# One-piece projections, a halved first block of x and a new table of thresholds in a two-attention kernel

## The chip, the cores and the metric

The kernel runs on one core of a Trainium2 chip. Five engines work side by side, each through its own queue in order: TensorE (PE) multiplies matrices into eight banks of PSUM, VectorE (DVE) and ScalarE (ACT) read those banks, GpSimd (POOL) works between on-chip tiles, and SyncE (SP) issues transfers. The metric is device time in microseconds (us) of one execution, the median of several. Before the change it is 1202.8 us in three runs (1199.12, 1202.80 and 1205.19).

## The reference, cut to what matters

Two attentions over 2048 positions and 512 features, each with 32 heads of 16 features, are computed from separate inputs, and their outputs stand side by side.

```python
# part A: softmax attention
q, k, v = split(x @ wqkv)                       # 32 heads of 16
p = softmax(q @ k.T * 16 ** -0.5)               # 2048 x 2048 for each head
a = concat_heads(p @ v) @ wo
# part B: linear attention with softmax feature maps
pq, pk = q @ w_phi, k @ w_phi                   # for each head 16 x 16
phi = lambda t: concat([softmax(t), softmax(-t)])
kv, z = phi(pk).T @ v, sum(phi(pk))
b = concat_heads(phi(pq) @ kv / (phi(pq) @ z + 1e-6)) @ wo
out = concat([a, b])
```

## The kernel before, in words

Part A is nearly all of the time. The work is cut into units: a group of four heads and 128 or 256 queries. There are eight groups, and each unit goes through three passes.

- **D pass.** `d_fill` multiplies keys with queries (line 971, 512 columns, half of PE's rows) into one PSUM bank, or two neighbouring banks at once. DVE then takes the maximum over the keys (line 1084): over one bank (512 elements, "128x1" in the profile, a single) or over two (1024 elements, "128x2", a pair). POOL joins the maxima (lines 1116 to 1122), and SP carries them by a transpose and two copies (lines 1134 and 1140) into the extra row of `QZ`, so that the next product already has the maximum taken off.
- **E pass.** `e_fill` multiplies again (line 1234), and ACT takes the exponential of one or two banks (line 1246) into a ring of tiles `pT`.
- **PV.** `pv_run` multiplies the exponentials with V (line 1324), four heads in four column strips of PE. A column of ones beside V gives the sums. The last three units take their sums with `ones_t` (line 1319) instead.

The projections of part A (`proj` and `proj8`), the output projection (`oproj`), and all of part B's matmuls are *jobs*: a list of pieces that PE runs between the passes. A piece is not broken up; between two pieces of a job passes may be put in. Before, a projection of four matmuls of 512 columns is two pieces of two.

The order of everything is set on the host while the program is built. A planner (`_Account`) keeps an account of when each engine comes free, by costs written in the code, and at each step chooses what each engine does next; what comes out is a fixed list of instructions for each engine, with the semaphore waits that the data need. What PE takes next depends on thresholds (`T`): above which lead of DVE and ACT a job's piece or PV may run (`COL`, `INCOL`), below which lead a single instead of a pair is taken (`SINGLE`, `ESINGLE`), when POOL, ACT and DVE share evacuations (`BAL`), and how busy PE must be kept (`UA`, `RF`, `LHARD`, `REPM`). Where PE would be too little busy by that account, the planner lets it repeat a D or E product (`again`) or multiply zeros (`fill_mm`, line 1854). The thresholds have one row for each 60 us of the account.

At the start, the first 512 rows of x come as two transfers (`load_x(0, ...)`, `load_x(1, ...)`). PE turns them by 16 matmuls with the identity (line 374) into four banks, one for each quarter of the features and 512 positions wide; then come two idle matmuls, and DVE and ACT evacuate two banks each (lines 381 and 383). The first projection of K and then that of Q (line 710) follow, 512 columns each; DVE makes the masked queries `QZ` of the first three units out of the bank of Q (line 734), and the D passes begin. From this point the planner orders everything.

## Time and profile before

| What | Value |
|---|---|
| Median of three runs | 1202.8 us |
| Time of the profiled execution | 1199.05 us |
| Its span, first to last instruction | 1197.3 us |
| DVE busy | 1170.3 us, 98% of the span |
| ACT busy | 1149.8 us, 96% |
| PE busy | 1117.4 us, 93% |
| POOL busy | 821.8 us, 69% |
| Granted TensorE clock, mean | 0.999 |

The profiled execution lies 3.75 us under the median of the runs. A row of the groups has line, engine, operation, tiles, shapes and count, then the busy time of all and the mean duration of one in ns, then the engine's idle time just before them. Instructions of one engine overlap a little at their ends, so durations of neighbours add up to more than the time between their starts. A row of the timeline has start, length, engine, line, what it does and how many follow each other; its shape is that of the first of them. A window row gives each engine's busy time within a stretch.

### The profile page before, as it was taken

The page shows a single profiled execution, that of the slowest core. Times are in us where ns is not written, and L with a number is a line of the kernel's source. Part 1 is how long each engine was busy: PE and PEld are TensorE (multiplying, and loading weights), DVE is VectorE, ACT ScalarE, POOL GpSimd, SP SyncE. Part 2 cuts the span into 40 slices and gives each one's busy share as a digit, 9 for nine tenths or more (in the row PEclk, how much of TensorE's full clock was granted, in tenths as well). Part 3 has the DMA queues.
Part 4 walks back from the last instruction along what each step waited for, and adds up shares of the span by engine and source line. Part 5 has one row for each costly group of instructions (what it writes and reads, how often), then busy time and mean ns, then how long its engine had stood idle before and what let it go on. Part 6 is the DMA issues. An engine that isn't in the chain of part 4 may idle for free.

```text
span 1197.3 us, 32106 instructions
## 1 busy us (share of the span) xinstructions
PE 1117.4 (93%) x13025; PEld 468.9 (39%) x13025; DVE 1170.3 (98%) x1290; ACT 1149.8 (96%) x1891; POOL 821.8 (69%) x1636
## 2 busy tenths in 40 slices
PE   8998999998999999999999998999999998899998
PEld 3433333343334333333433333333333333345555
DVE  8999999999999999999999999999999999999995
ACT  5898999999999999999999999999999999999997
POOL 8511211227888888888787887888888888888860
PEclk9999999999999999999999999999999999999999
DMA  5011221210002001001000101121112111111120
GB/s 142 9 25 43 42 48 32 43 38 8 8 14 35 8 6 26 13 10 22 12 7 17 25 7 22 22 49 31 29 34 33 35 34 27 20 29 37 33 30 18
DMA packets 104119, 33.61 MB, mean 28 GB/s; under 512 B 86692, under 2 KB 103972, under 8 KB 103972
## 3 DMA queue, kind: packets, MB, share of 16 engines
q1 hardware_dynamic: 102916, 31.31, 13.4%
q8 instruction: 102, 1.67, 0.6%
q14 instruction: 45, 0.37, 0.1%
q10 hardware_dynamic: 1056, 0.26, 0.1%
HBM read 5.26 MB, written 4.19 MB: 8 GB/s over the span
## 4 chain that ended last, share of the span: by engine, by line
ACT 38%; DVE 33%; PE 23%; SPq 2%; issue 1%; POOL 1%; DMA 1%
ACT pT L1246 32%; DVE part L1084 32%; PE PS L1234 7%; PE PS L971 6%; PE PS L1324 5%; PE PS L1419 2%; ACT eB L1639 1%; ACT xAT L560 1%; PE PS L777 1%; ACT zS L1011 1%; ACT X L560 1%; SPq L1392 1%; ACT WQp L560 1%; POOL uB L1588 1%; PE PS L1563 0%
## 5 line engine op out<-in xcount | busy, mean ns | idle before, releaser
L1084 DVE TENSOR_REDUCE part<-PS 128x2 f32<-128x1024 f32 (+1 forms) x1118 | 1130.0, 1079 | 7.6 <-PE PS L971 5.2
L1246 ACT ACTIVATE pT<-PS 128x512 bf16<-128x512 f32 (+1 forms) x1573 | 1027.7, 797 | 21.3 <-PE PS L1234 17.9
L1234 PE MATMUL PS<-QZ,KT 64*128 64x256 bf16 (+1 forms) x4906 | 560.4, 259 | 40.9 <-ACT pT L1246 22.0
L971 PE MATMUL PS<-KT,QZ 64*128 64x512 bf16 x2139 | 484.5, 383 | 26.3 <-DVE part L1084 9.7
L1234 PEld LDWEIGHTS PS<-QZ,KT 64*128 64x128 bf16 x4906 | 245.5, 94 | 323.1 <-ACT pT L1246 161.4
L971 PEld LDWEIGHTS PS<-KT,QZ 64*128 64x128 bf16 x2139 | 126.2, 93 | 198.2 <-DVE part L1084 72.2
L1324 PE MATMUL PS<-pT,VP 128*17 128x256 bf16 (+1 forms) x4672 | 186.7, 261 | 0.9
L1403 POOL TENSOR_TENSOR QT<-X,Yd 128x256 bf16<-128x256 f32 (+1 forms) x70 | 46.8, 668 | 95.4 <-DMA Yd<-Yd 95.1
L1324 PEld LDWEIGHTS PS<-pT,VP 128*17 128x17 bf16 x4672 | 74.9, 88 | 95.2 <-issue 79.0
L1588 POOL TENSOR_TENSOR uB<-uB 128x256 f32<-128x256 f32 (+2 forms) x160 | 83.4, 522 | 10.1
L1591 POOL TENSOR_SCALAR uB<-uB 128x256 f32<-128x256 f32 (+2 forms) x128 | 82.6, 646 | 11.2
L1116 POOL TENSOR_TENSOR dm<-part 128x16 f32<-128x16 f32 (+1 forms) x66 | 15.7, 238 | 91.1 <-DVE part L1084 90.8
L915 POOL TENSOR_TENSOR QZ<-QT,mask 128x512 bf16<-128x512 bf16 (+1 forms) x70 | 65.9, 941 | 15.7 <-PE PS L1234 12.8
L1645 POOL TENSOR_TENSOR xAT<-eB 128x512 f32<-128x512 bf16 x32 | 36.9, 1152 | 40.8 <-ACT eB L1639 40.6
L1677 POOL TENSOR_TENSOR wA<-eB,rB 128x1024 bf16<-128x1024 bf16 x32 | 61.7, 1928 | 2.0
L560 ACT ACTIVATE xAT<-PS 128x512 f32<-128x512 f32 (+3 forms) x83 | 50.1, 617 | 4.4 <-PE PS L1443 2.9
L1648 POOL TENSOR_TENSOR xAT<-xAT 128x256 f32<-128x256 f32 x64 | 36.0, 563 | 5.0
L1563 PE MATMUL PS<-WKp,xBT 128*128 128x512 bf16 x128 | 36.4, 383 | 1.1 <-ACT pT L1246 0.5
L1639 ACT ACTIVATE eB<-uB 128x1024 bf16<-128x1024 f32 x32 | 36.0, 1124 | 0.0
L1419 PE MATMUL PS<-WOp,QT 128*128 128x512 bf16 x120 | 35.8, 384 | 0.1
L1588 POOL TENSOR_TENSOR uB<-xAT,mB 128x512 f32<-128x512 f32 x32 | 33.8, 1057 | 1.8
L1662 POOL TENSOR_TENSOR WQp<-rB,WQp 128x64 f32<-128x64 f32 x96 | 30.6, 319 | 6.4
(113 smaller groups left out, 752.4 us busy)
## 6 DMA issues: line engine op xcount, KB each, us to landing
out_dram<-xAT SPq DMA_DIRECT2D x31, 128.0 KB, 1.8
Yd<-Yd SPq DMA_DIRECT2D x220, 16.0 KB, 2.1
QT<-eB SPq DMA_DIRECT2D x60, 32.0 KB, 2.0
QZ<-mcols SPq DMA_DIRECT2D x110, 1.0 KB
pT<-in_A_x_dram SPq DMA_DIRECT2D x3, 512.0 KB, 7.5
KT<-eB SPq DMA_DIRECT2D x48, 32.0 KB, 2.0
mcols<-stage SPq DMA_TRANSPOSE x69, 2.2
Yd<-Yd SPq DMA_DIRECT2D x60, 8.0 KB, 1.9
```

The costliest lines, as they stand in the source:

```text
L560: return P.op("act", lambda e: e.activation(dst, src, ACT.Copy), tk)
L915: "pool", lambda e: e.tensor_tensor(QZ[:, u % NQZ, :, 0:w], QT[:, g, q0:q0 + w].unsqueeze(1).broadcast_to([128, 2, w]), mask2[:, 0, :].uns ...
L971: return e.matmul(PS[:, b, :], QZ[p:p + 64, u % NQZ, r % 2, qt * 128:qt * 128 + 128], KT[p:p + 64, g, kc * 512:(kc + 1) * 512], start=star ...
L1084: tk = P.op("dve", lambda e: e.tensor_reduce(o, banks_ap(banks), AX.X, ALU.max), dep)
L1234: tok = P.op("pe", lambda e, r=rs[k], b=banks[k], kt=kt, x=x: e.matmul(PS[:, b, x * w:(x + 1) * w], KT[64 * (r // 2):64 * (r // 2) + 64, g ...
L1246: tk = P.op("act", lambda e: e.activation(pT[:, s0:s0 + n, :] if n > 1 else pT[:, s0, :], banks_ap(banks), ACT.Exp, scale=0.25), dep)
L1324: tok = P.op("pe", lambda e, r=r, kt=kt, x=x, s=es_[r][1]: e.matmul(PS[32 * r:32 * r + 17, bank, 0:w], VP[:, kt, 4 * g + r, :], pT[:, s, x ...
L1419: return e.matmul(PS[:, b, :], QT[:, i, st * 128:(st + 1) * 128], WOp[:, i, :], start=(i == 0), stop=(i == 7))
L1588: return P.op("pool", lambda e: e.tensor_tensor(o, a, b, op), dep)
L1591: return P.op("pool", lambda e: e.tensor_scalar(o, o, 0.0, None, ALU.max), dep)
L1639: cx["e"] = K.task("act", (0.95, 1.07), lambda eng: P.op("act", lambda e: e.activation(eB[:], uB[:], ACT.Exp), toks(d3)), d3, prio=-0.5, n ...
L1677: cx["phi"] = K.task("pool", (1.95, 1.95 + PLAT), lambda eng: P.op("pool", lambda e: e.tensor_tensor(phiB[k].rearrange("p (g f) -> p g f", ...
```

## The change

Four things are changed together.

1. Jobs of four matmuls that were two pieces of two become one piece of four: the eight-head projections of part A (`proj8`, 27 jobs), the feature maps of part B (`fm`, 32), the projection of V of part B (`v_job`, 16) and the output projection of part B (`ob_job`, 16). The projections in `proj` (the first K, Q and all V of part A) and `oproj` stay in pieces of two.
2. The first 512 rows of x are turned and evacuated in two halves of 256 positions, each after its own transfer, into eight banks in place of four. Q of the first 256 positions is projected by itself, right after the first half (four matmuls of 256 columns into bank 0), and `QZ` of the first two units is made from it; Q of the other 256 positions follows K as a job. The copy of the weights of Q into their padded place stands behind the first half of x on DVE. The two idle matmuls are gone.
3. The third transfer of x (`load_x(2, ...)`) waits until the first has landed. It is issued on SP's queue, and the weights and the later parts of x stand behind it there.
4. All 20 rows of the thresholds are replaced, and the account starts at 6.8 us in place of 7.6, with some arrival times moved by the same kind of amount.

```diff
-        def load_x(name, b0, b1):
+        def load_x(name, b0, b1, dep=()):
             t_xs[name] = P.dma("sp", dsem("xs%d" % name), lambda e: e.dma_start(
-                xs[:, b0:b1, :], A_x[0][128 * b0:128 * b1, :].rearrange("(b p) n -> p b n", p=128)))
+                xs[:, b0:b1, :], A_x[0][128 * b0:128 * b1, :].rearrange("(b p) n -> p b n", p=128)), list(dep))
...
-        load_x(2, 4, 8)
+        load_x(2, 4, 8, [t_xs[0]])
...
         pe_idle(6, [t_zmv, t_ones])
-        for rb in range(4):
+        t_x0 = {}
+        for hf in range(2):
+            for rb in range(2 * hf, 2 * hf + 2):
+                for ct in range(4):
+                    t_turn = P.op("pe", lambda e, rb=rb, ct=ct, hf=hf: e.matmul(
+                        PS[:, 4 * hf + ct, 128 * (rb % 2):128 * (rb % 2) + 128],
+                        xs[:, rb, ct * 128:ct * 128 + 128], ident[:, :],
+                        start=True, stop=True), [t_xs[hf], t_ident] if ct == 0 else [])
             for ct in range(4):
-                t_turn = P.op("pe", lambda e, rb=rb, ct=ct: e.matmul(
-                    PS[:, ct, 128 * rb:128 * rb + 128], xs[:, rb, ct * 128:ct * 128 + 128], ident[:, :],
-                    start=True, stop=True), [t_xs[rb // 2], t_ident] if ct == 0 else [])
-        pe_idle(2)
-        t_x0 = []
+                dst_x = xAT[:, ct, 256 * hf:256 * hf + 256]
+                src_x = PS[:, 4 * hf + ct, 0:256]
+                if ct % 2 == 0:
+                    t_x0[hf, ct] = P.op("dve", lambda e, o=dst_x, i=src_x: e.tensor_copy(o, i), [t_turn])
+                else:
+                    t_x0[hf, ct] = P.op("act", lambda e, o=dst_x, i=src_x: e.activation(o, i, ACT.Copy), [t_turn])
+            if hf == 0:
+                t_wqp = pad_copy(WQp, 0, t_wq0)
         for ct in range(4):
...
+            t_q0 = P.op("pe", lambda e, ct=ct: e.matmul(
+                PS[:, 0, 0:256], WQp[:, ct, 0, :], xAT[:, ct, 0:256], start=(ct == 0), stop=(ct == 3)),
+                [t_wqp, t_x0[0, 2], t_x0[0, 3]] if ct == 0 else [])
...
-            {'SINGLE': 1.013, 'ESINGLE': 1.026, 'ZBIAS': 0.274, 'DBIAS': 0.27, 'ZREST': 0.238},
+            {'SINGLE': 0.55, 'RF': 0.478, 'LHI': -0.049, 'JOBHOLD': 18.93, 'PVN': 2, 'ZBIAS': 0.053, 'ZREST': 0.028},
...
-        K.now = 7.6
+        K.now = 6.8
...
+                c0 = 256 if (kind, g, c) == ("q", 0, 0) else 0
...
+        held.add(0)
+        first_qz(0, T_q0, [0, 1])
         early = [("k", 0, 0), ("q", 0, 0)]
...
-            job(at, [(2, 512, mm), (2, 512, lambda e, b, i: mm(e, b, i + 2))], fin,
+            job(at, [(4, 512, mm)], fin,
                 T_xa[c] + [w8[kind]], prio)
...
-            job(K.now + 8.0, [(2, 512, mm), (2, 512, lambda e, b, i: mm(e, b, i + 2))], fin,
+            job(K.now + 8.0, [(4, 512, mm)], fin,
                 [BL[("xb", st // 4)], BL["wb"]], prio=K.now + 14)
```

Since the planner makes the whole order anew, nearly every row of every engine moves. The places that the prediction speaks of are these.

On PE, the start of the program. `pT` holds x as it came, `WKp` and `WQp` the weights of K and Q, `QZ` and `KT` are queries and keys of a D pass. Lines below 400 stand ahead of the planner. Before:

```order
L368 MATMUL PS<-zmv,ones_t 128x512 x6
L374 MATMUL PS<-ident,pT 128x128 x16
L368 MATMUL PS<-zmv,ones_t 128x512 x2
L710 MATMUL PS<-xAT,WKp 128x512 x4
L710 MATMUL PS<-xAT,WQp 128x512 x4
L807 MATMUL PS<-ident,pT 128x128 x12
L971 MATMUL PS<-KT,QZ 128x512 x4
L807 MATMUL PS<-ident,pT 128x128 x16
```

Now:

```order
L367 MATMUL PS<-zmv,ones_t 128x512 x6
L376 MATMUL PS<-ident,pT 128x128 x16
L390 MATMUL PS<-xAT,WQp 128x256 x4
L723 MATMUL PS<-xAT,WKp 128x512 x4
L723 MATMUL PS<-xAT,WQp 128x256 x4
L723 MATMUL PS<-xAT,WKp 128x512 x2
L986 MATMUL PS<-KT,QZ 128x512 x4
L723 MATMUL PS<-xAT,WKp 128x512 x2
L820 MATMUL PS<-ident,pT 128x128 x16
```

The first half of Q has moved ahead of K; the first four D products stand behind half a projection of K of the second group in place of 12 turns of x.

On DVE, the same place. `xAT` is the turned x, `part` takes the maxima. Before:

```order
L361 COPY WKp<-wA 128x4x8x16
L361 COPY WQp<-wA 128x4x8x16
L381 CAST xAT<-PS 128x512 x2
L734 TENSOR_TENSOR QZ<-PS,mask 128x2x128 x2
L734 TENSOR_TENSOR QZ<-PS,mask 128x512
L1084 TENSOR_REDUCE part<-PS 128x2 x13
```

Now:

```order
L361 COPY WKp<-wA 128x4x8x16
L384 CAST xAT<-PS 128x256 x2
L361 COPY WQp<-wA 128x4x8x16
L384 CAST xAT<-PS 128x256 x2
L747 TENSOR_TENSOR QZ<-PS,mask 128x2x128 x2
L747 TENSOR_TENSOR QZ<-PS,mask 128x512
L1099 TENSOR_REDUCE part<-PS 128x2 x2
L1099 TENSOR_REDUCE part<-PS 128x1 x2
```

Two casts of 512 have become four of 256 around the copy of Q's weights, and singles stand among the first maxima.

On PE, the end of the program, where the last E products stand. `woB` is the output weight of part B, `WOp` that of part A. Before:

```order
L1234 MATMUL PS<-QZ,KT 128x128 x8
L1813 MATMUL PS<-woB,xAT 128x512 x2
L1234 MATMUL PS<-QZ,KT 128x128 x16
L1813 MATMUL PS<-woB,xAT 128x512 x2
L1443 MATMUL PS<-WOp,QT 128x256 x14
L1234 MATMUL PS<-QZ,KT 128x128 x16
L1319 MATMUL PS<-pT,ones_t 32x128 x4
```

Now:

```order
L1458 MATMUL PS<-WOp,QT 128x256 x12
L1249 MATMUL PS<-QZ,KT 128x128 x8
L1458 MATMUL PS<-WOp,QT 128x256 x2
L1249 MATMUL PS<-QZ,KT 128x128 x8
L1334 MATMUL PS<-pT,ones_t 32x128 x4
```

Part B's last output projection has gone from here to before the last D pass, and the last E products stand apart from each other.

Counted over the whole program, the instructions that differ in number (lines as before) are:

| Engine, what | Before | Now |
|---|---|---|
| DVE maxima, singles (L1084, 128x1) | 276 | 246 |
| DVE maxima, pairs (L1084, 128x2) | 842 | 857 |
| DVE copies from PSUM of 272 and of 128 columns | 0 and 0 | 1 and 2 |
| ACT exponentials, singles (L1246, 128x512) | 1098 | 896 |
| ACT exponentials, pairs (L1246, 128x1024) | 475 | 576 |
| ACT copies from PSUM of 272 and of 128 columns into `WQp`, `X` | 32 and 15 | 31 and 13 |
| PE products of D (L971) | 2139 | 2077 |
| PE products of E (L1234) | 4906 | 4758 |
| PE products of zeros (L1854) | 100 | 364 |
| Jobs of the four kinds above whose four matmuls stand in a row | 26 of 91 | 91 of 91 |

D and E products are fewer because fewer are repeated; each maximum and each exponential is still taken once. POOL and SP have the same instructions in another order.

More of the change, by code (lines that the diff above doesn't have):

```diff
@@ L472, in bass_concat_heads__softmax_full_mha__linear_kernel_hedgehog__prompt_kernel @@
         free_banks = list(range(NBANK))
[L473 removed]
+        bank_tok = {4 * hf + ct: t_x0[hf, ct] for hf in range(2) for ct in range(4)}
+        free_banks.remove(0)
         pe_mode = [None]
```

85 lines of the change are left out of this document (40 added, 45 removed).

## The prediction

> **What bounds the kernel.** I read the page's busy times first, then the groups of instructions by shape, then the waits of DVE, and the windows by stage.
>
> ```profile
> PE 1117.4 (93%) x13025; PEld 468.9 (39%) x13025; DVE 1170.3 (98%) x1290; ACT 1149.8 (96%) x1891; POOL 821.8 (69%) x1636
> L1084 DVE TENSOR_REDUCE part<-PS 128x2 f32<-128x1024 f32 x842 | 971.1, 1211 | 6.9 <-PE PS L971 4.8 <-PE PS L978 0.2
> L1084 DVE TENSOR_REDUCE part<-PS 128x1 f32<-128x512 f32 x276 | 177.7, 676 | 0.7 <-PE PS L971 0.5
> L1246 ACT ACTIVATE pT<-PS 128x512 bf16<-128x512 f32 x1098 | 614.9, 674 | 4.6 <-PE PS L1234 2.4
> L1246 ACT ACTIVATE pT<-PS 128x1024 bf16<-128x1024 f32 x475 | 499.4, 1083 | 16.7 <-PE PS L1234 15.5
> ```
>
> DVE is the bound: 1170.3 of 1197.3 us, nearly all of it the maxima of line 1084, which waited for data only 6.9 + 0.7 = 7.6 us in 1118 instructions. ACT follows with 47.5 us idle. So the time is: DVE's start, its work, its few gaps, and what follows its last maximum. These windows show where its idle time lies.
>
> ```profile
> 0.00:10.00 10.00, 6.78 (x46) 3.25 (x48) 4.28 (x14) 3.41 (x5) 4.75 (x11) 1.00 0.85 255
> 60.00:120.00 60.00, 52.81 (x649) 21.08 (x641) 57.95 (x62) 53.84 (x81) 10.53 (x26) 1.00 0.14 34
> 660.00:720.00 60.00, 56.96 (x621) 23.07 (x616) 59.91 (x64) 59.40 (x107) 49.45 (x100) 1.00 0.09 16
> 1170.00:1198.00 28.00, 21.88 (x627) 14.53 (x623) 14.46 (x29) 20.45 (x32) 2.29 (x4) 0.96 0.08 18
> ```
>
> The third busy column is DVE: it idles 5.7 us in the first ten, 2.1 us around 60 to 120, 0.1 us in a typical stretch, and 13.5 us at the end. With 27.0 us idle in all, that leaves 27.0 − 5.7 − 13.5 = 7.8 us between. A schedule can win that and something at both ends, and no more, as long as DVE's work stays.
>
> **The change, term by term.** The sum is made against the profiled execution's own 1199.05 us, which is 3.75 us under the median of 1202.8; I add that back at the end.
>
> *DVE's work.* Thirty singles become fifteen pairs (the table of counts). What a pair and a single take in a stream is read from two unbroken runs of one shape.
>
> ```profile
> 10.69 14.79 DVE L1084 TENSOR_REDUCE part<-PS 128x2 f32<-128x1024 f32 x13
> 1170.43 3.67 DVE L1084 TENSOR_REDUCE part<-PS 128x1 f32<-128x512 f32 x6
> L1362 DVE TENSOR_TENSOR QT<-PS,Yd 128x128 bf16<-128x128 f32 x3 | 0.9, 286 | 0.1
> L563 DVE CAST xAT<-PS 128x256 bf16<-128x256 f32 x1 | 0.4, 424 | 0.8 <-PE PS L1443 0.8
> ```
>
> Thirteen pairs: (14.79 − 1.21) / 12 = 1.13 us each. Six singles: (3.67 − 0.68) / 5 = 0.60 us. Two singles less one pair is 0.07, times 15 is 1.0 us won. By the busy times of the two groups it is 2 × 0.644 − 1.153 = 0.135, so 2.0 us, a little too much since neighbours overlap. I take 1.5 us. Against it, DVE takes over three copies that ACT made: one of 272 columns (nearest row 0.42 us) and two of 128 (0.29), 1.0 us. Net −0.5 us, between −1.0 and 0. [...]
>
> *ACT's and PE's work.* 202 single exponentials become 101 pairs: by the groups' busy times 101 × (2 × 0.560 − 1.051) = 7 us less on ACT, plus 1 us of copies. ACT is not the bound, so this is nothing in the sum; it makes DVE's cover of 20 us of difference wider. On PE repeats go and zeros come:
>
> ```profile
> L971 PE MATMUL PS<-KT,QZ 64*128 64x512 bf16 x2139 | 484.5, 383 | 26.3 <-DVE part L1084 9.7
> L1234 PE MATMUL PS<-QZ,KT 64*128 64x256 bf16 (+1 forms) x4906 | 560.4, 259 | 40.9 <-ACT pT L1246 22.0
> L1854 PE MATMUL PS<-zmv,ones_t 128*17 128x512 bf16 x100 | 8.5, 384 | 2.2 <-DVE Yd L1356 1.1
> ```
>
> 62 × 0.227 + 148 × 0.114 = 31 us less, 264 × 0.085 = 22 us more: 9 us less of 1117. No term, since PE has 80 us to spare.
>
> *The start.*
>
> ```profile
> 4.24 0.65 PE L374 MATMUL PS<-ident,pT 128*128 128x128 bf16 x8
> 5.47 0.62 PE L374 MATMUL PS<-ident,pT 128*128 128x128 bf16 x8 [0.59 <-DMA pT<-in_A_x_dram]
> 5.84 0.29 DVE L361 COPY WQp<-wA 128x512 bf16<-128x512 bf16 x1 [0.93 <-DMA wA<-in_A_wqkv_dram]
> 6.13 1.29 DVE L381 CAST xAT<-PS 128x512 bf16<-128x512 f32 x2
> 7.48 1.04 PE L710 MATMUL PS<-xAT,WKp 128*128 128x512 bf16 x4 [0.95 <-DVE xAT L381]
> 8.55 0.69 ACT L559 ACTIVATE KT<-PS,bias_k 128x512 bf16<-128x512 f32 x1 [1.34 <-PE PS L710]
> 9.42 1.35 DVE L734 TENSOR_TENSOR QZ<-PS,mask 128x256 bf16<-128x256 f32 x3 [2.00 <-PE PS L710]
> 9.98 0.61 PE L971 MATMUL PS<-KT,QZ 64*128 64x512 bf16 x4
> ```
>
> The first maximum starts at 10.69. With the changed order on the same landings: the first half of x is turned by 4.9, DVE casts it (2 × 0.42) until 5.8 beside ACT, copies Q's weights until 6.1, and casts the second half from 6.1 to 7.0. K starts at 7.0 instead of 7.48, ends at 8.1, and ACT's 0.69 us end at 8.8. Ahead of it PE has put Q's first half in its idle time, and DVE makes the first two `QZ` from 7.0 to 7.8. Behind K, PE runs the other half of Q (to 8.6) and two matmuls of K (0.6 us, to 9.1), then the D products. Row 9.98 to row 10.69 is 0.7 us, but DVE was busy until then; two products take 0.4. The first maximum so starts at about 9.6: 1.1 us earlier. If the two transfers land 0.5 us earlier, because the third no longer runs beside them, it is 1.6.
>
> What is queued behind the new wait: the weights of V, the fourth and fifth part of x and the second weights of K and Q, all on SP.
>
> ```profile
> 0.79 1.49 SPq L329 DMA_DIRECT2D pT<-in_A_x_dram  x3
> 1.00:2.00 1.00, 0.33 (x1) 0.13 (x2) 0.94 (x3) 1.00 (x1) 0.56 (x2) 1.00 0.03 8
> 12.00:13.00 1.00, 1.00 (x6) 0.31 (x5) 1.00 (x2) 1.00 (x3) 0.94 (x2) 1.00 1.10 335
> 13.00:14.00 1.00, 1.00 (x12) 0.53 (x9) 1.00 (x2) 0.91 (x3) 0.93 (x3) 1.00 1.20 278
> ```
>
> The transfers (last columns of the windows: share and GB/s) are one stream, 335 GB/s as late as 12 to 13 us. The third part of x is issued at about 4.2 (when the turns of the first start) instead of about 1.8. In the meantime 768 KB (two parts of x of 256, two of weights of 128) keep the stream full until nearly 5 us. The first issue, at 0.79, moved next to nothing before 2, so an issue brings its first bytes about 1.2 us later, at 5.4: the stream has a hole of up to 0.6 us, and everything behind is that much later. DVE wants it 1.1 us earlier. So up to 1.5 us (0.6 and most of the 1.1) may be given back where PE stands at a turn of x with D products behind it. I take −1.1 us, between −1.6 and +0.4.
>
> *The pieces.* A projection now holds PE for four matmuls on end.
>
> ```profile
> 177.81 0.61 PE L777 MATMUL PS<-xAT,WQp 128*128 128x512 bf16 x2
> 178.35 0.39 PE L971 MATMUL PS<-KT,QZ 64*128 64x512 bf16 x2
> 608.73 1.04 PE L1563 MATMUL PS<-WKp,xBT 128*128 128x512 bf16 x4
> 609.70 0.39 PE L971 MATMUL PS<-KT,QZ 64*128 64x512 bf16 x2
> 610.13 2.35 DVE L1084 TENSOR_REDUCE part<-PS 128x2 f32<-128x1024 f32 x2 [0.29 <-PE PS L971]
> ```
>
> Such runs of four exist before: 26 of the 91. The worst of them gave DVE a gap of 0.29 us. The hole for DVE is 1.04 + 0.39 = 1.43 us against one pair of 1.13 in hand; with two banks more in hand there is none. Sixty-five more of them cost between 0 and 65 × 0.3 = 20 us. I take none: if each of the 26 had cost 0.3, that alone would be 8 us, more than the 7.6 us of waiting in the whole program.
>
> *DVE's other gaps.* The whole order is new, and the 7.8 us may shrink or grow. Nothing in the rows says which way; the term is 0, between −5 and the price of the rival below.
>
> *The tail.*
>
> ```profile
> 1176.23 12.21 ACT L1246 ACTIVATE pT<-PS 128x512 bf16<-128x512 f32 x16 [0.29 <-PE PS L1234]
> 1180.94 0.17 DVE L1164 TENSOR_REDUCE zS<-part 128x2 bf16<-128x8 f32 x1
> 1185.21 0.60 PE L1813 MATMUL PS<-woB,xAT 128*128 128x512 bf16 x2
> 1186.79 1.69 PE L1443 MATMUL PS<-WOp,QT 128*128 128x256 bf16 x14
> 1188.86 1.94 ACT L1246 ACTIVATE pT<-PS 128x1024 bf16<-128x1024 f32 x2 [0.41 <-PE PS L1234]
> ```
>
> From the last join of maxima (1180.94) to the end it is 16.4 us, set by ACT's exponentials. Before and after, 64 E products follow it; the 1.69 us of output projection that stood ahead of the last 16 and let ACT wait 0.41 us is now broken by 8 of them, and part B's two pieces are gone from here. In their place stands one more unit of PV, beside ACT's work. I take −0.5 us, between −1.5 and +1.5.
>
> *Sum:* −0.5 − 1.1 + 0 + 0 − 0.5 = −2.1 us: 1196.95 for such an execution, 1200.7 for the median.
>
> **Rivals.** Anything under 0.5%, 6 us, is about what a measurement of this kernel cannot tell from no change.
>
> *A: no more than the ends move.* This is the sum: 1200.7, from 1196 to 1206.
>
> *B: the new thresholds close DVE's gaps.* For it: ACT gets 7 us lighter and PE 9 us, and PE's waits for ACT's banks (22.0 us in the row of line 1234) delay D products too. Against it: at most 7.8 us are there. With 5 of them the time is 1200.7 − 5 = 1195.7, 0.6% faster; this is faster by over 0.5% once 3.9 us go.
>
> *C: pieces of four starve DVE (slower).* Place: behind each of the 91 jobs, between 50 us and the end. At 0.3 us for half of the 65 new ones it is 10 us: 1210.7. It decides from 8.1 us, at 0.125 us for each. For it: 1.43 us against 1.13 in hand. Against it: the 26 of before.
>
> *D: PE's clock falls (slower).* The page's clock row grants full speed everywhere but at the end, where the window shows 0.96.
>
> ```profile
> 1.68 2.74 PE L368 MATMUL PS<-zmv,ones_t 128*128 128x512 bf16 x6 [1.68 <-POOL zmv L316]
> 5.93 0.59 PE L368 MATMUL PS<-zmv,ones_t 128*128 128x512 bf16 x2
> ```
>
> The same matmul comes every 0.44 us at the start ((2.74 − 0.57) / 5, with the longer first) and 0.2 us later on, so PE can be half as fast. It is 93% busy: what it does in 10 us takes some 19 at half speed, so one such stretch gives 1200.7 + 9 = 1210, and 9 us of it decide. [...] Against it: 264 products of zeros are added, and no row of before shows such a stretch within the program.
>
> *E: the later transfers eat the start.* Then the sum is −0.6 and the time 1202, within 0.5%.
>
> **Numbers.** A 0.45 and E 0.07, both within 0.5%; B 0.26, faster; C 0.17 and D 0.05, slower. Faster 0.26, same 0.52, slower 0.22. A's own range is 1196 to 1206. The range reaches to B's full 7.8 us with both ends at their best (1202.8 − 1.0 − 1.6 − 1.5 − 7.8 = 1191) and to C and D: 1191 to 1211.
>
> **What would show it.** In the profile after: the first maximum near 9.6 us, not later than 10.3; DVE busy near 1170, its idle time near 25 us with some 8 between the ends; ACT 6 us less busy; the waits of line 1099 for line 986 near 5 us. C would show as gaps of 0.3 us behind runs of four matmuls; D as an 8 or less in the clock row; E as idle DVE between 12 and 20 us, ended by a transfer. The prediction is wrong if DVE's idle time between the ends goes beyond 16 us or below 4.

## The result, and the profile after

The changed kernel takes 1203.8 us (median of 20 runs, 1202.7 to 1205.9) against 1201.7 for the kernel before (20 runs, 1198.7 to 1205.2). The ratio is 1.002, 95% interval 1.0013 to 1.0027: 2.1 us slower, within 0.5%, where 2.1 us less was forecast. The range of 1191 to 1211 holds it.

The profiled execution after took 1204.14 us, with a span of 1202.4. These are the lines of the page and of the groups by shape that answer to those of before.

```profile
PE 1090.5 (91%) x13006; PEld 459.6 (38%) x13081; DVE 1173.3 (98%) x1279; ACT 1144.3 (95%) x1790; POOL 824.6 (69%) x1636
L1099 DVE TENSOR_REDUCE part<-PS 128x2 f32<-128x1024 f32 x857 | 988.9, 1212 | 10.7 <-PE PS L986 7.3 <-PE PS L993 0.4
L1099 DVE TENSOR_REDUCE part<-PS 128x1 f32<-128x512 f32 x246 | 159.5, 678 | 1.2 <-PE PS L986 0.2
```

ACT has 5.5 us less to do. PE's 27 us less are in part a matter of the records: here 75 of its 13081 matmuls are missing from the trace (x13006 beside x13081), and none in the first trace of before. DVE, the bound, has 15 maxima fewer and is busy 3.0 us longer, and its maxima wait 11.9 us in place of 7.6. The windows by stage (the third busy column is DVE) say where:

```profile
0.00:10.00 10.00, 7.83 (x49) 3.94 (x50) 6.12 (x18) 3.46 (x7) 4.81 (x11) 1.00 0.78 239
10.00:20.00 10.00, 9.75 (x77) 4.70 (x76) 8.63 (x11) 8.82 (x17) 9.86 (x15) 1.00 0.88 182
20.00:1170.00 1150.00, 1047.02 (x12197) 434.75 (x12272) 1138.76 (x1214) 1107.43 (x1735) 807.95 (x1609) 1.00 0.12 25
1170.00:1202.40 32.40, 25.87 (x704) 16.24 (x693) 19.76 (x40) 24.63 (x33) 1.98 (x3) 1.00 0.08 18
```

DVE idles 3.9 us in the first ten (5.7 before) and 1.4 in the next ten (0 before), 11.2 us from there to 1170 (8.4 before), and 12.6 behind that (12.8 before). These idle times and the work add up to the span, so the 5.1 us between the two traces are: start −0.5, middle +2.8, end −0.2, work +3.0. The medians differ by 2.1 us only, because the profiled execution of before lay 2.6 us under its median. That remainder turned out to be the most telling part, and the last experiments are on it.

**The start** in the timeline after, on DVE, ACT and PE:

```profile
9.08 4.68 DVE L1099 TENSOR_REDUCE part<-PS 128x2 f32<-128x1024 f32 x5
15.04 6.09 DVE L1099 TENSOR_REDUCE part<-PS 128x2 f32<-128x1024 f32 x6 [1.28 <-PE PS L986]
10.41 3.52 ACT L570 ACTIVATE xAT<-PS 128x512 bf16<-128x512 f32 x7
13.76 0.75 ACT L569 ACTIVATE KT<-PS,bias_k 128x512 bf16<-128x512 f32 x1
14.61 0.39 PE L986 MATMUL PS<-KT,QZ 64*128 64x512 bf16 x2
```

and the evacuation of the second 512 keys before:

```profile
13.27 0.69 ACT L559 ACTIVATE KT<-PS,bias_k 128x512 bf16<-128x512 f32 x1
```

The first maximum stands at 9.08, 1.6 us earlier than before. Five maxima later DVE has used up the first 512 keys. The second 512 keys are evacuated by ACT at 13.76, behind seven evacuations of turned x and half a microsecond later than in this trace of before, and the D products on them begin at 14.61, so DVE waits 1.28 us.

**Behind the jobs** DVE waits as rival C described, for example here:

```profile
614.01 1.04 PE L1728 MATMUL PS<-wA,xBT 128*128 128x512 bf16 x4
614.98 0.39 PE L986 MATMUL PS<-KT,QZ 64*128 64x512 bf16 x2
615.41 1.23 DVE L1099 TENSOR_REDUCE part<-PS 128x2 f32<-128x1024 f32 x1 [0.40 <-PE PS L986]
```

Fifteen gaps of 0.16 to 0.44 us, 4.1 us in all, stand behind jobs of four matmuls: nine directly, six with a few E products between. Before, gaps behind jobs came to some 1.5 us.

### The profile page after: what moved, and what is told of

Its sections match the earlier page's. It is cut to its first block, busy times and chain, and to the rows that moved or that the text cites. A ratio compares the mean times of both kernels' runs of the same rounds, so it can differ in the third digit from the quotient of the medians.

```text
span 1202.4 us, 32022 instructions
## 1 busy us (share of the span) xinstructions
PE 1090.5 (91%) x13006; PEld 459.6 (38%) x13081; DVE 1173.3 (98%) x1279; ACT 1144.3 (95%) x1790; POOL 824.6 (69%) x1636
## 3 DMA queue, kind: packets, MB, share of 16 engines
q1 hardware_dynamic: 102916, 31.31, 12.7%
## 4 chain that ended last, share of the span: by engine, by line
ACT 46%; PE 30%; DVE 18%; POOL 2%; issue 2%; SPq 1%; DMA 1%; POOLq 0%
ACT pT L1261 40%; DVE part L1099 17%; PE PS L1249 8%; PE PS L986 8%; PE PS L1339 7%; PE PS L1434 2%; ACT xAT L570 1%; ACT zS L1026 1%; ACT eB L1654 1%; PE PS L707 1%; ACT X L570 1%; PE PS L723 1%; PE PS L1578 1%; PE PS L790 1%; ACT WQp L570 1%
## 5 line engine op out<-in xcount | busy, mean ns | idle before, releaser
L1099 DVE TENSOR_REDUCE part<-PS 128x2 f32<-128x1024 f32 (+1 forms) x1103 | 1132.7, 1093 | 11.9 <-PE PS L986 7.5
L1249 PE MATMUL PS<-QZ,KT 64*128 64x256 bf16 (+1 forms) x4758 | 526.3, 259 | 50.6 <-ACT pT L1261 31.4
L986 PE MATMUL PS<-KT,QZ 64*128 64x512 bf16 x2077 | 458.9, 383 | 31.5 <-DVE part L1099 13.4
L1249 PEld LDWEIGHTS PS<-QZ,KT 64*128 64x128 bf16 x4758 | 224.6, 94 | 315.0 <-ACT pT L1261 155.9
L986 PEld LDWEIGHTS PS<-KT,QZ 64*128 64x128 bf16 x2077 | 119.8, 93 | 199.8 <-DVE part L1099 69.2
L1339 PE MATMUL PS<-pT,VP 128*17 128x256 bf16 (+1 forms) x4672 | 183.8, 261 | 2.6 <-ACT pT L1261 0.5
L1418 POOL TENSOR_TENSOR QT<-X,Yd 128x256 bf16<-128x256 f32 (+1 forms) x70 | 46.9, 670 | 97.8 <-DMA Yd<-Yd 97.6
L1606 POOL TENSOR_SCALAR uB<-uB 128x256 f32<-128x256 f32 (+2 forms) x128 | 82.9, 647 | 11.2
L570 ACT ACTIVATE xAT<-PS 128x512 f32<-128x512 f32 (+2 forms) x84 | 50.4, 620 | 5.6 <-PE PS L1458 4.0
L1869 PE MATMUL PS<-zmv,ones_t 128*17 128x512 bf16 (+1 forms) x364 | 34.1, 381 | 6.3 <-DVE Yd L1371 1.1
L1603 POOL TENSOR_TENSOR uB<-mB,xAT 128x512 f32<-128x512 f32 x32 | 33.9, 1059 | 2.3
```

The lines of the kernel that those rows point to most:

```text
L570: return P.op("act", lambda e: e.activation(dst, src, ACT.Copy), tk)
L986: return e.matmul(PS[:, b, :], QZ[p:p + 64, u % NQZ, r % 2, qt * 128:qt * 128 + 128], KT[p:p + 64, g, kc * 512:(kc + 1) * 512], start=star ...
L1099: tk = P.op("dve", lambda e: e.tensor_reduce(o, banks_ap(banks), AX.X, ALU.max), dep)
L1249: tok = P.op("pe", lambda e, r=rs[k], b=banks[k], kt=kt, x=x: e.matmul(PS[:, b, x * w:(x + 1) * w], KT[64 * (r // 2):64 * (r // 2) + 64, g ...
L1339: tok = P.op("pe", lambda e, r=r, kt=kt, x=x, s=es_[r][1]: e.matmul(PS[32 * r:32 * r + 17, bank, 0:w], VP[:, kt, 4 * g + r, :], pT[:, s, x ...
L1418: return P.op("pool", lambda e: e.tensor_tensor(QT[:, g, q0:q0 + w], X[:, ub, 0:w], Yd[:, ub, 0:w], ALU.mult), toks(d5) + [pt.tok])
```

## Experiments

Two kinds of kernels were made. In the first, the planner runs as it is and the order that comes out is written down; then only the instructions named are moved, and the semaphore waits are worked out again for the new order. In the second, one input of the planner is changed and it makes the whole order anew. Ratios are against runs of before on the same chip.

| Run | Kernel and edit | Median, us | Ratio (95%) |
|---|---|---|---|
| e1 | after's order, 46 jobs split by a D pass | 1213.4 | 1.0102 (1.0088 to 1.0116) |
| e2 | before's order, halves of 65 jobs joined | 1216.4 | 1.0125 (1.0109 to 1.0141) |
| e3 | after without the wait of the third load | 1203.5 | 1.0018 (1.0010 to 1.0027) |
| e4 | after with the old thresholds | 1229.1 | 1.0233 (1.0219 to 1.0246) |
| e5 | before with the pieces of four alone | 1216.5 | 1.0130 (1.0112 to 1.0148) |
| e6 | before, account starts at 7.61, not 7.60 | 1223.9 | 1.0190 (1.0165 to 1.0216) |
| e7 | after's order, one projection later | 1204.8 | 1.0021 (1.0012 to 1.0031) |
| e8 | after's order, 22 D passes earlier | 1206.3 | 1.0039 (1.0025 to 1.0052) |
| e9 | e7 and e8 | 1208.4 | 1.0054 (1.0041 to 1.0066) |
| e10 | before with the new thresholds alone | 1222.8 | 1.0177 (1.0163 to 1.0191) |
| e11 | after's order, the 25 late D passes earlier | 1210.2 | 1.0069 (1.0057 to 1.0082) |
| e12 | after's order, nine jobs split at a gap | 1205.2 | 1.0031 (1.0022 to 1.0041) |
| e13 | before's order, ten loads later on SP | 1198.0 | 0.9971 (0.9960 to 0.9983) |

### Pieces, with the order held (e1, e2)

```diff
         K.loop(pick_pe, choose, more)
+        P.replay(split_log(P.log))
...
+                if to is not None and log[to][5]:
+                    moved.setdefault(to, []).extend(ns[2:])
```

`P.log` is the list of instructions as planned, `to` the last product of the next D pass, `ns` the job's four matmuls.

> The changed kernel with its own order of instructions on every engine, but in 46 of the 91 jobs of four (those where the next pass on PE is a D pass, ahead of the job's evacuation) the last two matmuls are moved behind that D pass. Nothing is planned anew. Theory P (pieces of four keep the D product from DVE; 15 gaps of 4.1 us in all stand behind jobs in the changed kernel's trace): the gaps behind these jobs go, time 2 to 4 us (0.2 to 0.35%) under the changed kernel. Theory O (the loss lies in the new order as a whole, and the length of a piece is only where it shows): within 1 us of the changed kernel.

In e2, in the kernel before, the second two matmuls go behind the first two:

```diff
+                if pe_between:
+                    after[ns[1]] = ns[2:]
```

> The kernel before with its own order, but in the 65 jobs whose two halves stand apart on PE the second half is moved forward to the first, so that all 91 jobs are four matmuls in a row. Nothing is planned anew. Theory P: 65 more pieces at 0.05 to 0.1 us each, 3 to 6 us (0.25 to 0.5%) slower than before. Theory O: within 1 us of before.

Both fell on the slow side of every expectation: splitting jobs that had been planned in one piece cost 9.6 us, and joining jobs that had been planned in two cost 15 us. Neither size of piece is the better one in an order that was made for the other. The group of the maxima in e2, and that of a trace of before taken later (c2, below), show that not all of it is idle time:

```profile
L1129 DVE TENSOR_REDUCE part<-PS 128x2 f32<-128x1024 f32 (+1 forms) x1118 | 1135.5, 1082 | 18.4 <-PE PS L1014 12.2 <-PE PS L1279 1.8 <-PE PS L1021 0.2
```

```profile
L1084 DVE TENSOR_REDUCE part<-PS 128x2 f32<-128x1024 f32 (+1 forms) x1118 | 1130.9, 1082 | 10.3 <-PE PS L971 7.7 <-PE PS L978 0.2
```

These are the same 1118 instructions at the same mean duration of 1082 ns, 1209.7 us when added up. In before they overlap at their ends by 1209.7 − 1130.9 = 78.8 us, in e2 by 74.2. A maximum that stands right behind another instruction here overlaps it by some 0.08 us (before's 13 pairs from 10.69 us take 1.21 us each and start every 1.13); one that starts only when the engine has come to rest does not, and that counts as busy time. In e2's trace 101 maxima start with no overlap, in that of before 56: 45 more at 0.08 us are 3.6 of the 4.6 us. These 4.6 us are a part of e2's loss, beside 8.1 us more of waiting.

### The wait of the third load (e3)

```diff
-        load_x(2, 4, 8, [t_xs[0]])
+        load_x(2, 4, 8)
```

> The changed kernel without the wait of the third transfer of x for the first; the planner takes fixed arrival times, so the order stays the same. If the wait helps the first half of x: the first maximum starts later than 9.08 us, by up to 0.5, and the time is 0 to 0.5 us longer. If it costs (the later transfers are late and make the gap of 1.28 us at 15 us): that gap goes and the time is up to 1.3 us shorter.

The time is after's within 0.3 us, the first maximum stays at 9.08 us and the gap at 15.04 at 1.28 us. The wait on SP's queue neither cost nor won anything that shows. Since e3 keeps after's order, its trace is a second one of that order, and it is used as such below:

```profile
L1099 DVE TENSOR_REDUCE part<-PS 128x2 f32<-128x1024 f32 (+1 forms) x1103 | 1132.8, 1095 | 11.8 <-PE PS L986 7.7
20.00:1170.00 1150.00, 1049.52 (x12212) 435.74 (x12285) 1139.06 (x1215) 1108.17 (x1737) 805.67 (x1610) 1.00 0.12 25
```

### Tables and courses (e4, e5, e6, e10)

In e4 the 20 old rows stand in the changed kernel; in e10 the 20 new ones in the kernel before. In e5 and e6 the kernel before keeps its rows. The first lines are e4 (e10 is the reverse, on the kernel before; 20 rows each), the second e5 (with its like in the other three kinds of job), the third e6.

```diff
-            {'SINGLE': 0.55, 'RF': 0.478, 'LHI': -0.049, 'JOBHOLD': 18.93, 'PVN': 2, 'ZBIAS': 0.053, 'ZREST': 0.028},
+            {'SINGLE': 1.013, 'ESINGLE': 1.026, 'ZBIAS': 0.274, 'DBIAS': 0.27, 'ZREST': 0.238},
...
-            job(0.0, [(2, 512, mm), (2, 512, lambda e, b, i: mm(e, b, i + 2))], fin, deps, prio=K.now + 5)
+            job(0.0, [(4, 512, mm)], fin, deps, prio=K.now + 5)
...
-        K.now = 7.6
+        K.now = 7.61
```

> The changed kernel with the thresholds of before, planned anew: 270 single and 845 paired maxima, 808 single and 620 paired exponentials. Theory T (the new table fits the new code, a table made for other code does not): slower than the changed kernel by 5 us or more. Theory O (any other plan of the same work falls within a scatter of a few us): within 4 us of the changed kernel, either side.

> The kernel before with its start and its table of thresholds; only the 91 jobs are given to the planner as one piece of four, and the order is planned anew. It has 304 single and 828 paired maxima. Theory F (the table is fitted to one exact course of the plan; what costs is the misfit, not the length of a piece): 10 us or more slower than before, like the changed kernel with the old table (27.8 us over before in the run above). Theory P (a piece of four costs by its length alone, some 0.2 us for each of the 65 that are newly in a row): 10 to 15 us. The two differ in the next run.

> The kernel before, with the one change that the planner's account starts at 7.61 us in place of 7.60. The same work, the same pieces of two, the same start and table; the order comes out another way (364 single and 798 paired maxima, for 276 and 842). Theory F: 10 us or more slower, though nothing but the course of the plan is changed. Theory P, and the view of the prediction that DVE's gaps stay as they are when the order is made anew: within 4 us of before, apart from 44 pairs more that fell into two singles, 3 to 6 us.

> Before with the new table of thresholds alone; pieces of two, the old start, order planned anew. Theory F (a table fits one course of the plan and is worth nothing on another): 15 to 30 us slower than before, like the changed kernel with the old table (1229.1). Rival N (the new table is the better one, and pieces or start take its gain away): 1195 to 1201. Rival O (tables matter little): within 5 us of before.

Each of the two tables works with the code for which it was made and not with the other: old code with old table 1201.7, new with new 1203.8, but old with new 1222.8 and new with old 1229.1. Even 0.01 us in the start of the account cost 22 us. So the 15 us of e5 need be no price of pieces of four: a departure that changes no piece cost more. With all of the change's code the old table cost 25 us over the new one. The waits of DVE in e10 and e4 (total, number, longest, in us) show the form of the loss:

```profile
DVE part L1084 <- PE PS L971: 22.5, 32, 7.2
```

```profile
DVE part L1099 <- PE PS L986: 20.4, 48, 3.6
```

D products come late, in all 15 to 17 us more of waiting than in the first trace of before (5.2). In e10 most of it lies in three waits, of 7.2, 4.3 and 2.6 us; in the longest PE runs E products, PV and jobs ahead of the D product. This is another form than the many short gaps of the changed kernel.

### Mending single places (e7, e8, e9, e11, e12)

In e7 the first keys of the second group are projected and evacuated behind the second block's first D pass. One thing differs from what was meant: the moved projection now writes into a bank that still holds turned x, so some of the keys are wrong numbers in e7 and e9. The instructions and their sizes are the same.

```diff
+        if n == d:
+            out_ += [new[i] for i in ks + [ev] + px]
```

`d` is that D pass, `ks` and `ev` the projection and its evacuation, `px` the turn of x that uses the bank next.

> After's own order, fixed as it came out, with one projection moved: the first 512 keys of the second group (four matmuls of PE, and their evacuation of 0.69 us on ACT that stands ahead of the second block of x) go behind the first D pass on the second 512 keys. Nothing else moves; no instruction is added or left out. Theory S (the DVE gap of 1.28 us at 15 us is made by this evacuation and by its matmuls, which hold up the turned second block of x and so its keys): the gap falls to between 0.3 and 0.7 us, the whole time falls by 0.5 to 1.0 us against after, and the first maximum stays at 9.08 us. Rival T (the keys of the second block are limited by the transfer of x): the gap stays above 1.1 us and the time is after's within 0.3 us. Theory F (the table fits one exact course, and whatever moves costs): the gap falls, but the whole time rises by 2 us or more.

DVE there:

```profile
9.34 4.68 DVE L1143 TENSOR_REDUCE part<-PS 128x2 f32<-128x1024 f32 x5
14.88 1.23 DVE L1143 TENSOR_REDUCE part<-PS 128x2 f32<-128x1024 f32 x1 [0.86 <-PE PS L1028]
18.20 2.42 DVE L1143 TENSOR_REDUCE part<-PS 128x1 f32<-128x512 f32 x3 [2.10 <-PE PS L1028]
```

The gap shrank from 1.28 to 0.86 us, part of it since the first maximum came 0.26 us later, and a second gap of 2.10 us opened three microseconds on, behind the evacuation that had been moved. None of the three theories held: the gap is longer than S allows and shorter than T says. The time is 1204.8 us beside after's 1203.8, but as a ratio to before on the same chip it is 1.0021 beside 1.0020, so neither S's gain nor F's 2 us is there.

e8 was to move the late D passes. Its list of places had counted the second instruction of each maximum with `zS` as a maximum too, so from the second gap on it moved D passes that stand one to 22 maxima behind the late ones. It is thus a test of moves at places that needed none. `es` is the D pass, `to` the start of the stretch ahead of it:

```diff
+        es = [e for e in new[first:last + 1] if e[1] == "pe" and e[6] == ("D",)]
+        rest = [e for e in new[to:last + 1] if not any(e is d for d in es)]
+        new[to:last + 1] = es + rest
```

> After's own order, fixed as it came out, with 22 D passes moved: each one whose maximum DVE waited for in the trace of after (0.16 to 0.91 us each between 69 and 1058 us, 6.1 us in all) goes ahead of the one stretch of PE's work that stood before it (a job's four matmuls, E products, PV or idle products). Nothing is added or left out. Theory L (each gap is a single D pass that stands a little too late): these gaps go, 3 to 6 us of the whole time with them, 1198 to 1201. Theory F (the order is in balance as it stands; what a D pass gains, the E products behind it lose): the gaps at these places go, others open elsewhere, and the time is between 1 us less and 8 us more than after.

> Both moves together in after's order. If both gains are local, they add: the sum of the differences of the two runs before it, within 0.5 us, and at best 1197 to 1200, below before's 1201.7. If departures feed on each other, it is over 1 us away from that sum, on the slow side.

Of the 25 gaps of after between 69 and 1150 us, three went, one grew by 0.12 us, and the others stayed to 0.04 us. Eight new ones of 0.15 to 0.49 us opened, 1.9 us in all, and the time rose by 2.5. e9 is 1.1 us over the sum of the two, on the slow side, as the expectation has it for departures that feed on each other. With the places right, e11 moves the 25 passes themselves, and e12 splits only the nine jobs that have a gap directly behind them (`d` is the D pass):

```diff
+        half = [new[es[2]], new[es[3]]]
+        new[d + 1:d + 1] = half
```

> After's own order, fixed, with 25 D passes moved: those whose maximum ended the 25 gaps of DVE between 69 and 1150 us in the trace of after (7.3 us in all), each ahead of the one stretch of PE's work that stands before it. In the run that moved 22 others, the gaps of after stayed where they were to 0.02 us, and the two late passes that it happened to move lost theirs. Theory L (a gap is one D pass that stands too late): 20 or more of the 25 gaps go, and 3 to 7 us with them: 1197 to 1201. Theory F (what D gains there, the E products and the banks behind lose): fewer than 4 us of gaps in all go, since others open, and the time is within 2 us of after's 1203.8.

> After's own order, fixed, with the last two of the four matmuls moved behind the late D pass in those nine jobs where a gap of DVE (0.16 to 0.44 us, 2.6 us in all) stands right behind the job: pieces of two again, but only where DVE was seen to wait. Theory C (pieces of four starve DVE at these places): the nine gaps go and 2 to 4 us of the time with them, 1200 to 1202. Theory F (any move of the fixed order costs, as in the run that split 46 jobs): the nine gaps may go, but the time does not fall below 1203.

In e11, 18 of the 25 gaps went and 27 others opened; DVE's gaps for D products together grew from 8.6 to 11.5 us, and the time by 6.4 us, more than the 2 us that theory F allows too. In e12 seven of the nine went and eleven opened, most of them one to four maxima further on; the time rose by 1.4 us, a rise that the intervals of the two ratios (1.0022 to 1.0041, and after's 1.0013 to 1.0027) do not tell from none. One place as an example, first after, then e12 (PE, then DVE; of the job's four matmuls in the first line one record is missing):

```profile
154.90 0.81 PE L790 MATMUL PS<-xAT,WQp 128*128 128x512 bf16 x3 [0.32 <-ACT pT L1261]
155.65 0.39 PE L986 MATMUL PS<-KT,QZ 64*128 64x512 bf16 x2
149.00 6.87 DVE L1099 TENSOR_REDUCE part<-PS 128x2 f32<-128x1024 f32 x6
156.08 2.59 DVE L1099 TENSOR_REDUCE part<-PS 128x2 f32<-128x1024 f32 x2 [0.22 <-PE PS L986]
```

```profile
153.82 0.60 PE L832 MATMUL PS<-xAT,WQp 128*128 128x512 bf16 x2
154.36 0.39 PE L1028 MATMUL PS<-KT,QZ 64*128 64x512 bf16 x2
154.69 0.60 PE L832 MATMUL PS<-xAT,WQp 128*128 128x512 bf16 x2
149.27 6.88 DVE L1143 TENSOR_REDUCE part<-PS 128x2 f32<-128x1024 f32 x6
156.59 1.23 DVE L1143 TENSOR_REDUCE part<-PS 128x2 f32<-128x1024 f32 x1 [0.45 <-PE PS L1028]
```

The D pass that was late now stands between the halves of the job, its maximum follows without a gap, and the next maximum waits 0.45 us where the gap had been 0.22. Theories L and C fell: these gaps are not single passes at a wrong place, and most of what goes at one place comes back within a few maxima.

### Before's own scatter (c1, c2, e13)

The kernel before was profiled twice more, unchanged.

> The kernel before once more, unchanged, for a second trace: the profiled execution of before (1199.05) lay 2.6 us under its median. If the difference between the traces of before and after is the change's, a trace of before nearer its median (1200 to 1203) has the same idle time of DVE by stretches to 0.5 us and its busy time within 1 us of 1170.3. If it is scatter of the executions, DVE's busy time is 1171.5 or more, or its idle time between 20 and 1170 us 1 us above 8.4.

> A third trace of before, for the same question and with the same bounds: DVE's busy time and its idle time between 20 and 1170 us beside 1170.3 and 8.4.

They took 1202.1 and 1202.6 us. DVE's busy time is 1170.9 and 1171.1 us, within 1 us of the first trace; its idle time from 20 to 1170 us is 10.3 and 11.1, not 8.4. So most of the work is the change's, and the idle time in the middle scatters, nearly all of it at one place. First the middle of the second trace; then, from the third, the timeline of SP, PE and DVE and the windows with the granted clock (0.64 and 0.51, ahead of the last two columns):

```profile
20.00:1170.00 1150.00, 1064.87 (x12155) 445.04 (x12229) 1139.69 (x1235) 1115.27 (x1836) 807.74 (x1608) 1.00 0.13 25
```

```profile
90.83 1.38 SPq L1476 DMA_DIRECT2D BD<-in_B_w_phi_dram  x3
92.25 0.42 SPq L1480 DMA_DIRECT2D woB<-in_B_wo_dram  x1
92.72 1.12 SPq L1140 DMA_DIRECT2D QZ<-mcols  x2
96.24 0.61 PE L1234 MATMUL PS<-QZ,KT 64*128 64x256 bf16 x4 [2.01 <-DMA QZ<-mcols]
97.31 0.61 PE L971 MATMUL PS<-KT,QZ 64*128 64x512 bf16 x2
97.96 1.23 DVE L1084 TENSOR_REDUCE part<-PS 128x2 f32<-128x1024 f32 x1 [2.74 <-PE PS L971]
```

```profile
94.00:98.00 4.00, 1.99 (x24) 0.52 (x16) 1.26 (x3) 1.45 (x2) 0.00 (x0) 0.64 0.58 147
98.00:102.00 4.00, 4.00 (x40) 1.04 (x38) 3.03 (x3) 2.22 (x3) 1.72 (x2) 0.51 0.39 125
```

Loads of part B's weights stand on SP ahead of the copies of the maxima, and PE waits 2.0 us for these. Its clock falls to half (0.50 in the window from 98 to 100 us) during the wait, at 95.1 us, and stays there until 101.9: the same two D products take 0.61 us in place of 0.39. DVE loses 4.1 us here in four gaps. In the first trace PE waited 1.3 us at this place, its clock stayed at 1.00, and DVE lost 1.4 us; in the second it waited 2.1 us, the clock fell to 0.50, and DVE lost 3.2. After has no wait of PE longer than 0.9 us between 10 and 1170 us. e13 takes the wait away by moving ten transfers on SP's queue, nothing else:

```diff
         K.loop(pick_pe, choose, more)
+        P.replay(loads_later(P.log))
...
+    go = [n for n in sp if lo < n < hi and log[n][6] == ("load",)]
+        if n == to:
+            out_ += [log[i] for i in go]
```

`hi` is the copy of the maxima, `to` the fifth transfer behind it.

> Before's own order, fixed, with ten transfers moved on SP's queue alone: nine small loads of the feature map weights and the load of part B's output weight, issued between 81 and 91.8 us, go behind the copies of the maxima into the extra row (issued at 91.8 us in the first trace of before, 92.7 in the third) and the five transfers after them. No other engine's order changes. In the three traces of before PE waits 1.3, 2.1 and 2.0 us for these copies at 95 us; in the second and third its clock is then granted at 0.50 for some 4 us, and DVE loses 1.4, 3.2 and 4.1 us there. Theory W (this wait is what spreads before's times and lies in its median): PE's wait goes or falls under 0.5 us, no slice of the clock falls below 0.9 between 90 and 110 us, DVE's gap there is under 0.5 us, and the median is 1197 to 1199.5, 2 to 4 us under before and over 4 under after. Rival V (the maxima come late from POOL or DVE, not from SP's queue): the wait stays above 1 us and the time is before's within 0.7 us. Rival F (what moves costs): the wait goes, but the time is above before's.

```profile
88.67 1.11 SPq L1186 DMA_DIRECT2D QZ<-mcols  x2
94.44 0.39 PE L1280 MATMUL PS<-QZ,KT 64*128 64x256 bf16 x4
89.70 14.99 DVE L1130 TENSOR_REDUCE part<-PS 128x2 f32<-128x1024 f32 x13
```

```profile
0.00:10.00 10.00, 7.55 (x38) 3.65 (x39) 3.83 (x13) 3.06 (x4) 4.66 (x11) 1.00 0.87 254
20.00:1170.00 1150.00, 1067.68 (x12227) 447.55 (x12299) 1142.77 (x1243) 1119.28 (x1844) 807.44 (x1609) 1.00 0.13 25
1170.00:1196.20 26.20, 20.65 (x608) 13.85 (x608) 13.54 (x27) 19.38 (x30) 1.83 (x3) 0.98 0.08 19
```

Theory W held in all its numbers. The copies are issued 4.0 us earlier than in the third trace, PE does not wait, DVE runs 13 pairs without a gap, and the time is 1197.95 us (seven runs, 1197.5 to 1198.1): 3.6 us under before and 5.8 under the changed kernel. It beats both, and its seven runs spread over 0.6 us where eleven of before beside them spread over 4.4. So before's scatter was, nearly all of it, this one wait and the clock behind it. The clock that each run lists fits: of 60 runs of before beside the experiments, the nine with a mean of 1.000 took 1198.8 to 1200.7 us, the ten with 0.996 took 1202.2 to 1204.1.

With it the account of the change can be made. DVE, in us:

| | Before, first trace | Before, second | Before, third | e13 | After | e3 (after's order) |
|---|---|---|---|---|---|---|
| idle, 0 to 10 | 5.7 | 6.3 | 5.9 | 6.2 | 3.9 | 3.8 |
| idle, 10 to 20 | 0 | 0 | 0 | 0 | 1.4 | 1.4 |
| idle, 20 to 1170 | 8.4 | 10.3 | 11.1 | 7.2 | 11.2 | 10.9 |
| idle behind 1170 | 12.8 | 12.8 | 12.9 | 12.7 | 12.6 | 12.6 |
| busy | 1170.3 | 1170.9 | 1171.1 | 1170.2 | 1173.3 | 1173.1 |
| span | 1197.3 | 1200.3 | 1200.9 | 1196.2 | 1202.4 | 1201.8 |

Against before without its late transfer the change loses 6.2 us: the start gives 0.9, the middle takes 4.0, the work takes 3.1, the end stays. The median of before hides 3.6 us of this, since the changed order does not have that late transfer. Against the second trace, which is the nearest to before's median, it loses 2.1 us, as the medians do: the start gives 1.0, the middle takes 0.9, the work takes 2.4, and the end gives 0.2.

## Why the prediction was wrong

- *What bounds the kernel:* right. DVE's idle time and work by stage account for each of the spans above.
- *DVE's work, −0.5:* this is the step that failed. Busy time was taken as the number of instructions times a length from an unbroken run, as if the new order fed DVE as closely as the old one. The counts were right, but the term came out at +2.2 to +3.1 (1173.3 against 1170.2 to 1171.1). Against before's second trace, the nearest to its median, it missed by 2.9 us (+2.4 for −0.5), of the 4.2 us between the forecast of −2.1 and the measured +2.1. e3's trace, with after's order, has the same mean lengths of the two shapes as before's second and third (1214 and 679 ns): its maxima are busy for 1132.8 us, before's for 1130.9. So 1.9 us come with the change; between the first traces of the two kernels the means differ by 1 to 2 ns besides, and that scatters.
- *What came in the place of that step:* by unbroken runs, fifteen pairs for thirty singles should have given 1.0 us less. But in the two traces of after's order 81 and 76 maxima start with no overlap, in the three of before and in e13's 50 to 56. At 0.08 us each (1.21 less 1.13), the 20 to 31 more are 1.6 to 2.5 us of work, an estimate from these counts; maxima that lose a part of the overlap add 0.4 us between the first traces of the two kernels, and the rest is not settled.
- *ACT's and PE's work:* ACT came out 5.5 us lighter, where 8 were worked out with the copies. PE's 27 us, where 9 were worked out, come down to 15.6 against the second trace of before (1106.1), which lacks 78 matmul records where after lacks 75. Neither is in the sum, rightly.
- *The start, −1.1:* the first maximum came earlier still (9.08, not 9.6), and 1.28 us were given back at 15 us, so −0.5 remained against the first trace and −0.9 against e13. The reason given for what might be given back, the later transfers of rival E, fell with e3: there the gap stands without the wait. What ends the gap is the D products behind ACT's evacuation of the second block of keys, at 13.76 after and at 13.27 in the first trace of before; DVE started 1.6 us sooner on the first block, and the second did not.
- *The pieces, 0:* the signature of rival C is there, fifteen gaps of up to 0.44 us, but they come to 4.1 us against some 1.5 before: 2.6 us more, a quarter of C's price. That they are the price of pieces of four is not shown: e12 splits nine of them and gains nothing.
- *DVE's other gaps, 0:* this failed beside it, and the medians hide it. The prediction said that nothing in the rows tells which way they go, and took the middle. Against the first trace, for which the sum was made, the idle time from 20 to 1170 us grew by 2.8 us, against e13 by 4.0; against the second and third by 0.9 and 0.1 only, because there the late transfer costs the old order about as much as the new order's short gaps cost it. Both terms failed on the same thing: D products come late more often in the new order. Eight runs that depart from an order that was fitted, or use its table on another course (e1, e2, e4 to e6, e8, e10, e11), are slower than the kernel they start from, by 2.5 to 25 us; e12's 1.4 us are not clear. (e13, which moves transfers on SP alone and no work of an engine, is the one that gains.) No order that was made anew here came below the old one. Why the changed order has more late D products than the old one is not shown.
- *The tail, −0.5:* −0.2 against the first trace, 0 against e13.
- *The base:* the sum was made against an execution in which DVE lost 1.4 us at 96 us, and 3.75 us were added back as scatter of no known kind. That scatter was for the most part a wait in the old order that the new one does not have; so it should not have been carried over whole. It is luck that this error and those of the two terms above ran against each other: against the trace of the sum the terms missed by 7.2 us, against the medians by 4.2. A smaller slip is the last window, which ran to 1198 us and so 0.7 us past the end of the span: DVE idled 12.8 us there, not 13.5, and 8.4 between the ends, not 7.8.
- *Rival D* was rejected since "no row of before shows such a stretch within the program". That was one execution. In the two others of before the clock does fall, at 95 to 98 us (0.50 from 98 to 100 in both), and in e3, with after's order, it falls at 816.8 us for 3.4 us (a mean of 0.68 from 815 to 820). Its price was far from the 9 us worked out: from 20 to 1170 us DVE idles 10.9 us in e3 and 11.2 in after, whose clock there was 1.00. That products of zeros hold the clock up, for which the 264 of them were set against this rival, is not shown; in e2 it fell with PE busy for 0.84 to 1.00 of each microsecond from 458 to 463 (below).

The prediction's own bounds for being wrong (idle between the ends beyond 16 us or below 4) were not crossed: it is 12.6 us.

## What to carry to other kernels

A list of instructions that was tuned as a whole carries its value in the fit: price any change that makes the order anew as a loss until the tuning is shown to have been repeated, and expect a table of thresholds to lose its worth on another course (15 to 25 us here). Look at more than one trace before choosing a base: where runs spread by 0.5%, find the one wait that differs between a fast and a median execution; here, moving ten small loads behind an urgent copy on one queue was worth more than the whole change. And a wait on the bounding engine cost more here than its idle time: each maximum that started from rest also gave up some 0.08 us of overlap (1.21 less 1.13), which shows as busy time.

## What the runs showed of the hardware

PE's clock halved in some of these traces, at one place (e2, at 463.8 us) with no wait of PE over 0.2 us in the six microseconds ahead, and the length of a wait did not tell when. In before's second trace it fell to 0.50 at 97.8 us, 1.1 us behind a wait of 2.1, for 3.4 us; in the third at 95.1 us, 0.9 us into a wait of 2.0, for 6.8 us. A wait of 1.3 us in the first trace left it at 1.00, and so did one of 1.8 us at the same place in e2 (the wait in total, number, longest; then PE's window there: busy, clock, transfers):

```profile
PE PS L1279 <- DMA QZ<-mcols: 1.8, 1, 1.8
95.00:100.00 5.00, 3.70 (x62) 1.00 0.56 143
```

In e2 it fell at another place, with no wait longer than 0.2 us in the six microseconds ahead:

```profile
462.00:463.00 1.00, 0.90 (x8) 1.00 0.05 8
463.00:464.00 1.00, 0.80 (x7) 0.92 0.30 71
464.00:465.00 1.00, 1.00 (x7) 0.50 0.33 73
...
469.00:470.00 1.00, 1.00 (x14) 0.50 0.18 38
470.00:471.00 1.00, 1.00 (x15) 0.66 0.00 0
```

PE was busy for 0.84 to 1.00 of each microsecond from 458 to 463 and still ran at half speed from 463.8 to 470.7. In the traces named here no wait of PE ahead of a fall was longer than 2.1 us. What sets a fall off is not shown: neither the longest wait nor PE's busy share tells the places with a fall from those without.
